# RWKV recurrence and routed experts on one core: VectorE's order of a unit, and a dV split over two engines

## The chip, the cores and the metric

The kernel runs on one core of a Trainium2 chip. Its engines take instructions in order, each from its own queue: TensorE (PE; PEld is its weight load), VectorE (DVE), ScalarE (ACT), GpSimd (POOL), and SyncE (SP), which issues most transfers. They wait for one another through semaphores. The metric is device time in microseconds (us).

## The reference

All data are float32. The first part is a recurrence over 768 steps for 4 sequences and 8 heads of 48 columns; the second sends each of the 3072 resulting rows (384 columns) to one of eight experts.

```python
for t in range(S):
    cur = np.einsum('bhd,bhe->bhde', u[None] * kt, vt)
    y[:, :, t] = np.einsum('bhd,bhde->bhe', rt, state + cur)
    state = wt[:, :, :, None] * state + np.einsum('bhd,bhe->bhde', kt, vt)
...
logits = x @ w_gate + modality_bias[modality_id]
e_idx = np.argmax(logits, axis=1)
...
    h = np.maximum(x[mask] @ w1[e], 0.0)
    out[mask] = gate_w[mask, None] * (h @ w2[e])
```

## The kernel before

**Units.** The steps are cut into chunks of 128. A unit is one chunk of one sequence with all heads: 24 units, six to a sequence. Within a unit the recurrence becomes matrix products. The decays are multiplied up from the middle of the chunk outwards, in both directions, so that K (keys) and R (receptances) carry them. Then, on TensorE: `pS` = K times R (L362), masked to the earlier steps by VectorE (`A`, L364); the state `pU` (L376), which ScalarE scales (L379) and copies (`SPb`, L382); and `pY`, the output, from the state (L392) and from A (L401). The step's own term is `delta` (L289), copied to `dT`, times v: `dV`. VectorE adds pY and dV into the row tile `xp` (`x_rows`, L427), which TensorE transposes (`x_cols`, L434) for the expert logits (L440).

**Passes.** `att_iter(i)`, i from -2 to 23, emits the work of one pass for all engines. In pass i VectorE works the scans of unit a = i + 2 (K and R), the mask of unit m = i + 1 and the rows of unit z - 1 = i - 1; TensorE works pK, pS, delta and pU of unit m and pY of unit z = i; GpSimd prepares unit a + 1. The order of the Python lines is the order of each engine's queue. GpSimd's work in a pass is: `decays` (products of neighbouring decays into `pw`, L249), `keys` (`G` = r times k, L254), `dV` of unit z (L324), `within` (two in-place products of `in`, the K half first, L267). `on_vec(n, k)` says for which units VectorE does without a product by GpSimd: there `spread` takes three operations (L273 to L275) instead of one (L277). That is so for units 0 and 1, and for K in the six `busy` passes 15 to 20. In these, GpSimd issues the scatters of the first twelve units, two to a pass (L655), and ScalarE makes dV head by head (`half_dv`, L314, four heads to a call).

**Buffers.** `BE`, in which a scan leaves its result, lies in PSUM, and so do `pY`, `pS` and `T["R"]` (`pR`, logits and the routing's small tables). pY and pS have one buffer each: pS of the next unit can be written when the mask has read it, pY of the next when `x_rows` has. `in` has four buffers, K two, R, G and pw three.

**Setup and routing.** Small pieces run at the ends of passes as `hooks`: `setup_a` to `setup_d` and `guesses` in passes 2 to 6 (biases of the two modalities, and a guess which two experts come first), the routing of the first twelve units in passes 13 to 17 (`route_a`, `hook_b` with `route_b`, `table(0)`). `hook_b` emits the rank matmuls (L499) ahead of L401 and VectorE's ranks (L509 to L515); after it the scatters may start. `split_some` in the last two passes prepares the first expert's weights.

**Experts.** The first two blocks of 512 rows are loaded when the twelve scatters have landed (`blk_load`), transposed (`blk_t`, L687) and worked by TensorE in three passes of split precision (L701, L718). Work of the second half's routing runs in between.

Of the kernel before, what the change touches and what calls it, by code (L numbers as in the profile page):

```python
# [9 lines left out]
F32 = mybir.dt.float32  # L10
# [4 lines left out]
ALU = mybir.AluOpType  # L15
# [3 lines left out]
P = 128  # L19
# [34 lines left out]
GW = B * H * S * D // (P * NG)  # L54
WHALF = FC // 2 * DM
DRAIN_FROM = WB
NEARLY = 2
SCATTER = NJ + 3
EARLY = 6
NPW = 3  # L60
# [3 lines left out]
def kernel(ctx: ExitStack, tc: tile.TileContext, rkw, vt, wf, cst, mid, wg, bias, w1, w2, out):  # L64
# [111 lines left out]
    m1 = cp.tile([P, 2, NU], F32, name="m1")  # L176
    bt2 = raw[0][:, 0, 0:NU * E].rearrange("p (a e) -> p a e", a=NU)
    bv = bb.rearrange("p (a e) -> p a e", a=2)
    mx = cp.tile([P, 2], F32, name="emx")
    ec = cp.tile([P, 2, E], F32, name="ec")  # L180

    def setup_a():
        nc.scalar.copy(out=trib, in_=mask)
        nc.scalar.copy(out=mf, in_=mi[:, 0:2 * P:2])
        nc.scalar.copy(out=ersb[0:1], in_=ers[0:1])
        nc.scalar.copy(out=rcol(C_VEC + 3 * E, 1), in_=zt[:, 0:1])
        nc.gpsimd.tensor_copy(out=tidi, in_=tid)

        nc.vector.tensor_reduce(out=mx, in_=bv, axis=AX.X, op=ALU.max)
        nc.vector.tensor_tensor(out=ec, in0=bv, in1=mx[:, :, None].to_broadcast([P, 2, E]), op=ALU.is_equal)  # L190
        nc.gpsimd.tensor_tensor(out=ec, in0=ec, in1=i8[:, None, :].to_broadcast([P, 2, E]), op=ALU.mult)

    def bias_part(s, t):
        nc.gpsimd.tensor_tensor(out=t, in0=m1[:, s, :, None].to_broadcast([P, NU, E]),
                                in1=bb[:, None, s * E:(s + 1) * E].to_broadcast([P, NU, E]), op=ALU.mult)

    def setup_b():

        pm = rcol(C_VEC, NU)
        nc.tensor.transpose(out=pm, in_=mf, identity=ident[0:NU, 0:NU])  # L200
        nc.scalar.copy(out=m1[:, 1], in_=pm)
        nc.gpsimd.tensor_scalar(out=m1[:, 0], in0=m1[:, 1], scalar1=-1.0, scalar2=1.0, op0=ALU.mult, op1=ALU.add)
        bias_part(0, biasT)
        nc.vector.tensor_reduce(out=em, in_=ec, axis=AX.X, op=ALU.min)
        for ef, eo, op in ((e0f, oh0, ALU.min), (e1f, oh1, ALU.max)):
            nc.vector.tensor_tensor(out=ef, in0=em[:, 0:1], in1=em[:, 1:2], op=op)
            nc.gpsimd.tensor_tensor(out=eo, in0=ef.to_broadcast([P, E]), in1=i8, op=ALU.subtract)
            nc.gpsimd.tensor_tensor(out=eo, in0=eo, in1=eo, op=ALU.mult)
            nc.gpsimd.tensor_scalar(out=eo, in0=eo, scalar1=-1.0, scalar2=1.0, op0=ALU.mult, op1=ALU.add)
            nc.gpsimd.tensor_scalar(out=eo, in0=eo, scalar1=0.0, scalar2=None, op0=ALU.max)  # L210
            nc.gpsimd.tensor_scalar(out=ef, in0=ef, scalar1=float(E), scalar2=None, op0=ALU.add)
        nc.gpsimd.tensor_copy(out=e0i, in_=e0f)

    def guesses():
        ts, tt = nc.gpsimd.tensor_scalar, nc.gpsimd.tensor_tensor
        ts(out=row0, in0=e0f, scalar1=float(RS), scalar2=-float(DUMMY), op0=ALU.mult, op1=ALU.add)
        nc.vector.tensor_tensor(out=thr, in0=e0f, in1=e1f, op=ALU.is_equal)
        ts(out=row1, in0=thr, scalar1=float(BW), scalar2=-float(DUMMY), op0=ALU.mult, op1=ALU.add)
        ts(out=em[:, 0:1], in0=e1f, scalar1=float(RS), scalar2=None, op0=ALU.mult)
        tt(out=row1, in0=row1, in1=em[:, 0:1], op=ALU.add)  # L220
        ts(out=tab[:, 2, 1:2], in0=thr, scalar1=-1.0, scalar2=1.0, op0=ALU.mult, op1=ALU.add)
        ts(out=thr, in0=thr, scalar1=1.0, scalar2=None, op0=ALU.add)
        nc.gpsimd.tensor_copy(out=tab[:, 0, 1:2], in_=e1f)
        nc.gpsimd.tensor_copy(out=tabe[:, 1:2], in_=e1f)
# [22 lines left out]
    def decays(n, eng):  # L247
        w = sides(ins[n % NIN][:, 1024:LIN])
        eng.tensor_tensor(out=heads(pw[n % NPW])[:, :, 2:SEG - 1], in0=w[:, :, 0], in1=w[:, :, 1], op=ALU.mult)  # L249
# [6 lines left out]
    def busy(i):  # L256
        return SCATTER <= i < SCATTER + NJ // 2

    def on_vec(n, k):
        return n < NEARLY or (k == 1 and busy(n - 2))  # L260

    def within(n):
        t = ins[n % NIN]
        for k in (1, 0):
            if not on_vec(n, k):
                v = sides(t[:, 512 * k:512 * (k + 1)])[:, :, 1 - k]
                nc.gpsimd.tensor_tensor(out=v, in0=v, in1=sides(t[:, 1024:LIN])[:, :, k], op=ALU.mult)  # L267

    def spread(n, tag, src, c0, bufs=None):
        X = sides(wt(n, tag, [P, 4, P], bufs).rearrange("p a b -> p (a b)"))  # L270
# [11 lines left out]
    def ok(n):  # L282
        return 0 <= n < NU
# [21 lines left out]
    def rows_op(a):  # L305
        scan(pw[a % NPW], 1)
        spread(a, "R", ins[a % NIN][:, 0:512], 1, 3)

    def att_iter(i):
# [4 lines left out]
                nc.scalar.activation(out=dV[:, h], in_=v0[:, h], func=AF.Copy, scale=dT[:, h:h + 1])  # L314

        if ok(a + 1):
            if a + 1 >= NEARLY:
                decays(a + 1, nc.gpsimd)
            keys(a + 1)
        if ok(z):  # L320
            dV = wt(z, "dV", [P, H, D], 2)
            v0, dT = T["v", z].rearrange("p (a b) -> p a b", a=H), T["dT", z].rearrange("p a b -> p (a b)")
            if not busy(i):
                nc.gpsimd.tensor_tensor(out=dV, in0=v0, in1=dT[:, :, None].to_broadcast([P, H, D]), op=ALU.mult)  # L324
        if ok(a + 1):
            within(a + 1)
        if ok(z - 1):
            x_rows(z - 1)
        if ok(a):
            t, W = ins[a % NIN], wt(a, "W", [P, 4], 2)  # L330
            if a < NEARLY:
                decays(a, nc.vector)
            pp, n = pw[a % NPW], 4 * SEG
            scan(pp, -1)
            spread(a, "K", t[:, 512:1024], 3)
            nc.vector.reciprocal(out=pp[:, 1:n:SEG], in_=BE[:, 2:n:SEG])
            nc.vector.tensor_copy(out=W, in_=BE[:, 2:n:SEG])
            if a < NEARLY:
                rows_op(a)
        if ok(m):  # L340
            K, R, v = T["K", m], T["R", m], T["v", m]
            last, cont = first(m + 1), not first(m)
            if not last:
                pK = pt(("k", m), "pK")
                for p in range(4):
                    nc.tensor.transpose(out=pK[:, p * P:(p + 1) * P], in_=K[:, p], identity=ident)
                if m < NEARLY:
                    warm(NWARM[1 + 2 * m])
                nc.scalar.copy(out=KT, in_=pK.rearrange("p (a h b) -> p a h b", a=4, h=2))
        if ok(z - 2):  # L350
            x_cols(z - 2, pt(("x", z), "pX" if i == NU - 1 else "pT"))
        if ok(z) and busy(i):
            half_dv(0)
        if i == SCATTER:
            route_x(0)
        if ok(m):
# [8 lines left out]
            delta(m)  # L365
            if m == 0:
                warm(NWARM[2])
        if NEARLY <= a < NU:
            rows_op(a)
        if ok(m) and not last:  # L370
            if not cont:
                T["U"] = pt(m, "pU", (P, 4, D))
# [24 lines left out]
        if ok(z):  # L397
            for h in range(H):
                p, hh = divmod(h, 2)
                for q in (0, 64):  # L400
                    nc.tensor.matmul(out=pY[q:q + 64, h * D:(h + 1) * D], lhsT=A[:, hh, p, q:q + 64], rhs=v[:, h * D:(h + 1) * D],  # L401
                                     start=(first(z) and h == 0), stop=True, skip_group_check=True)
            if busy(i):
                half_dv(1)
        if i > SCATTER:
            split_some(i)

# [111 lines left out]
    def table(ph):  # L519
# [56 lines left out]
        if ph == 0:  # L576
            rounded(g, ct, 1.0 / BW, -0.5 + 0.5 / BW)
            s0 = wt("s", "s0", [P, 2], 1)
            vec.scalar_tensor_tensor(out=fA, in0=g, scalar=1.0, in1=oh0, op0=ALU.min, op1=ALU.mult)
            vec.tensor_reduce(out=s0[:, 0:1], in_=fA, axis=AX.X, op=ALU.add)  # L580
            ts(out=tab[:, 1, 0:1], in0=s0[:, 0:1], scalar1=row0, scalar2=float(DUMMY), op0=ALU.mult, op1=ALU.add)
            yield
            vec.scalar_tensor_tensor(out=sA, in0=g, scalar=thr, in1=oh1, op0=ALU.is_ge, op1=ALU.mult)
            vec.tensor_reduce(out=s0[:, 1:2], in_=sA, axis=AX.X, op=ALU.add)
            ts(out=tab[:, 1, 1:2], in0=s0[:, 1:2], scalar1=row1, scalar2=float(DUMMY), op0=ALU.mult, op1=ALU.add)
            tt(out=fA, in0=fA, in1=sA, op=ALU.add)
            return
        if ph == 1:
            rounded(g, ct, 1.0 / BT, -0.5 + 0.5 / BT)
            vec.scalar_tensor_tensor(out=g, in0=fA, scalar=-2.0, in1=g, op0=ALU.mult, op1=ALU.add)  # L590
            sums(cu, g)
            taken(sA, cu, 1)
            ts(out=fA, in0=fA, scalar1=2.0, scalar2=None, op0=ALU.mult)
            yield
            yield from rows(SA, 1, cu, None, fA)
            tt(out=fA, in0=fA, in1=sA, op=ALU.add)
            ts(out=sA, in0=fA, scalar1=0.5, scalar2=None, op0=ALU.mult)
            return
# [500 lines left out]
```

## Time and profile before

| | |
|---|---|
| median of 3 runs | 364.48 us (364.15 to 364.69) |
| the profiled execution | 364.56 us |
| its span, first to last instruction | 362.3 us |
| mean granted TensorE clock | 0.993 |
| busy: PE, PEld | 347.5 us (96%), 314.1 us (87%) |
| busy: DVE, ACT, POOL | 234.5 us, 193.3 us, 154.4 us |

Rows of the order of time give start and length in us, engine, line, operation, `out<-in` by the program's names, the shape, and how many instructions are merged in the row; in brackets stands the idle time of the engine before it and what ended it. A VectorE instruction's length overlaps the next one's start a little, so costs in a chain are read from start to start. Rows of stretches give, after the bounds and the length, each engine's busy time, the granted clock, the DMA share and GB/s.

### The profile page before, as it was taken

How to read it: one execution, taken by the hardware profiler on the slowest of the kernel's cores; microseconds unless marked ns; L12 is line 12 of the kernel's file. 1: busy time of each engine (PE TensorE's matmuls, PEld its weight loads, DVE VectorE, ACT ScalarE, POOL GpSimd, SP SyncE). 2: the span in 40 equal slices, each digit the busy share in tenths (PEclk: the TensorE clock that was granted, in tenths of full speed). 3: DMA queues.
4: the chain of work that ended last, by engine and by line, in shares of the span. 5: the costliest groups of instructions: out<-in, count | busy, mean ns of one | idle time of the engine just before them, and what ended most of it. 6: DMA issues, size and time to landing. Idle time of an engine off the chain costs nothing.

```text
span 362.3 us, 9892 instructions
## 1 busy us (share of the span) xinstructions
PE 347.5 (96%) x3900; PEld 314.1 (87%) x3900; DVE 234.5 (65%) x481; ACT 193.3 (53%) x436; POOL 154.4 (43%) x201
## 2 busy tenths in 40 slices
PE   8899889999898999999999999999999999999993
PEld 3699789999797887799889999889988998899993
DVE  7999799999998955698756276335434443535330
ACT  2464465365758764361349565439525852665340
POOL 4898999995488863013761210201210220022021
PEclk9999999999989999999999999999999999999999
DMA  7966977786676350006330543504680566020010
GB/s 252 388 218 167 305 258 240 237 301 208 238 237 218 107 177 3 0 2 240 141 145 0 198 153 90 174 0 104 243 307 2 145 217 248 1 67 27 5 44 26
DMA packets 19612, 55.53 MB, mean 153 GB/s; under 512 B 2501, under 2 KB 10603, under 8 KB 19556
## 3 DMA queue, kind: packets, MB, share of 16 engines
q1 hardware_dynamic: 16420, 45.34, 38.1%
q0 software_dynamic: 3136, 9.47, 6.9%
q8 instruction: 32, 0.52, 0.6%
q14 instruction: 24, 0.20, 0.2%
HBM read 58.69 MB, written 12.03 MB: 195 GB/s over the span
## 4 chain that ended last, share of the span: by engine, by line
PE 56%; issue 7%; DVE 6%; ACT 4%; DMA 3%; POOLq 1%; POOL 0%; DVEq 0%; ACTq 0%
PE pS_u L701 25%; PE pY_d L718 13%; PE pX_d L718 13%; DVE pX_s L303 1%; DMA xs<-xp,posT 1%; ACT pU L379 1%; DMA xl<-xs 1%; ACT dV L314 1%; PE pK_x L687 1%; PE pU_x L687 1%; ACT SPb L382 1%; DVE A L364 1%; PE pY L401 1%; PE pT_x L687 1%; DVE K L273 1%
## 5 line engine op out<-in xcount | busy, mean ns | idle before, releaser
L726 POOL DMA_INDIRECT out<-ot,xl x25 | 26.2, 1047 | 171.9 <-ACT ot L725 147.1
L244 DVE TENSOR_TENSOR wl<-raw,wh 128x768 fp32r<-128x768 f32 x56 | 52.6, 956 | 42.7 <-ACT wh L243 41.4
L706 DVE SCALAR_TENSOR_TENSOR hl<-pS_u,hh 128x512 fp32r<-128x512 f32 x48 | 33.2, 691 | 53.4 <-ACT hh L705 53.4
L705 ACT ACTIVATE hh<-pS_u 128x512 fp32r<-128x512 f32 x48 | 28.7, 598 | 62.9 <-PE pS_u L701 62.9
L701 PE MATMUL pS_u<-xh,wl 128*128 128x512 f32 (+1 forms) x168 | 61.3, 365 | 0.0
L701 PE MATMUL pS_u<-xh,wh 128*128 128x512 f32 (+1 forms) x168 | 61.0, 363 | 0.0
L701 PE MATMUL pS_u<-xo,wh 128*128 128x512 f32 (+1 forms) x168 | 60.9, 363 | 0.0
L243 ACT CAST wh<-raw 128x768 fp32r<-128x768 f32 (+1 forms) x64 | 49.4, 800 | 13.8 <-PE pX_d L718 13.8
L701 PEld LDWEIGHTS pS_u<-xo,wh 128*128 128x128 f32 x168 | 31.5, 188 | 5.4
L701 PEld LDWEIGHTS pS_u<-xh,wh 128*128 128x128 f32 x168 | 31.6, 188 | 5.1
L701 PEld LDWEIGHTS pS_u<-xh,wl 128*128 128x128 f32 x168 | 31.5, 188 | 5.2
L303 DVE TENSOR_TENSOR_SCAN pX_s<-pw,pX_s 128x268 f32<-128x268 f32 x48 | 34.1, 710 | 0.1
L362 PE MATMUL pS<-R,K 64*128 64x128 f32 x384 | 27.9, 285 | 6.2 <-DVE R L277 5.1
L254 POOL TENSOR_TENSOR G<-in 128x512 f32<-128x512 f32 x24 | 31.5, 1311 | 5.3 <-DMA in<-rkw 5.3
L655 POOL DMA_INDIRECT xs<-xp,posT x24 | 25.3, 1053 | 19.6 <-DVE xp L515 8.3
L362 PEld LDWEIGHTS pS<-R,K 64*128 64x128 f32 x384 | 23.3, 187 | 11.5 <-DVE R L277 7.5
L718 PE MATMUL pY_d<-wh,hh 128*128 128x384 f32 x96 | 33.0, 343 | 0.0
L718 PE MATMUL pX_d<-wh,hh 128*128 128x384 f32 x96 | 32.3, 337 | 0.0
L718 PE MATMUL pY_d<-wl,hh 128*128 128x384 f32 x96 | 32.3, 336 | 0.0
L718 PE MATMUL pY_d<-wh,hl 128*128 128x384 f32 x96 | 32.3, 336 | 0.0
L718 PE MATMUL pX_d<-wl,hh 128*128 128x384 f32 x96 | 32.3, 336 | 0.0
L718 PE MATMUL pX_d<-wh,hl 128*128 128x384 f32 x96 | 32.3, 336 | 0.0
(409 smaller groups left out, 708.2 us busy)
## 6 DMA issues: line engine op xcount, KB each, us to landing
raw<-w SPq DMA_DIRECT2D x28, 768.0 KB
in<-rkw SPq DMA_DIRECT2D x22, 768.0 KB
v<-vt SPq DMA_DIRECT2D x24, 192.0 KB
wg<-wf SPq DMA_DIRECT2D x8, 576.0 KB
xl<-xs SPq DMA_DIRECT2D x5, 772.0 KB
raw<-w SPq DMA_DIRECT2D x8, 384.0 KB
xs<-zt SPq DMA_DIRECT2D x8, 193.0 KB
in<-rkw SPq DMA_DIRECT2D x6, 256.0 KB
```

Source lines behind the costliest of these rows:

```text
L243: nc.scalar.copy(out=wh[k][:, sl], in_=raw[k][:, sl])
L244: (eng or (nc.vector, nc.gpsimd)[k]).tensor_tensor(out=wl[k][:, sl], in0=raw[k][:, sl], in1=wh[k][:, sl].bitcast(F32), op=ALU.subtract)
L254: nc.gpsimd.tensor_tensor(out=G, in0=t[:, 0:512], in1=t[:, 512:1024], op=ALU.mult)
L303: nc.vector.tensor_tensor_scan(out=BE[:, ::step], data0=pp[:, ::step], data1=d1[:, ::step], initial=0.0, op0=ALU.mult, op1=ALU.max)
L362: nc.tensor.matmul(out=pS[:, hh, p], lhsT=K[q, p], rhs=R[q, p], start=True, stop=True)
L655: rows_apart("xs", nc.gpsimd.indirect_dma_start(out=xs[:, :], out_offset=bass.IndirectOffsetOnAxis(ap=posT[:, n:n + 1], axis=0), in_=T["xb ...
L687: nc.tensor.transpose(out=pp[:, c - c0, j * P:(j + 1) * P], in_=xl[:, j, c * P:(c + 1) * P], identity=ident)
L701: nc.tensor.matmul(out=pp[:, i], lhsT=wsrc[0][:, f, c * P:(c + 1) * P], rhs=xsrc[:, c, 0:w], start=(n == 0), stop=(n == 3 * KC - 1))
L705: nc.scalar.activation(out=hh, in_=pp, func=AF.Relu)
L706: nc.vector.scalar_tensor_tensor(out=hl, in0=pp, scalar=0.0, in1=hh.bitcast(F32), op0=ALU.max, op1=ALU.subtract)
L718: nc.tensor.matmul(out=X["y", q, j], lhsT=hsrc[:, j * P:(j + 1) * P], rhs=wsrc[1][:, f], start=(f == 0 and n == 0), stop=(f == FC - 1 and ...
L726: ins = nc.gpsimd.indirect_dma_start(out=out[:, :], out_offset=bass.IndirectOffsetOnAxis(ap=xl[:, j, DM + 1:DM + 2].bitcast(I32), axis=0), ...
```

## The change

VectorE's order in a pass becomes: both scans of unit a with K and R, then the rows of unit i - 1, then the mask of unit i + 1 (before: rows, scan, K, mask, scan, R). `dV` is halved in every pass that is not busy: ScalarE makes heads 0 to 3, GpSimd heads 4 to 7. In busy passes ScalarE's second half moves ahead of the scaling of pU. The decay of unit 1 goes to GpSimd. R of unit 1 is prepared by GpSimd, K of unit 2 no more. The two in-place products of `within` become one instruction over both halves. In the setup, two small tiles move to PSUM, `thr` is made there instead of in `guesses`, and one sum of `table(0)` moves to `table(1)`.

```diff
-NEARLY = 2
+NEARLY = 3
@@ setup_a
+        mx = rcol(C_VEC, 2)
         nc.vector.tensor_reduce(out=mx, in_=bv, axis=AX.X, op=ALU.max)
@@ setup_b
+        e2 = rcol(C_VEC + NU + 1, 2)
         nc.vector.tensor_reduce(out=em, in_=ec, axis=AX.X, op=ALU.min)
+        nc.vector.tensor_copy(out=e2, in_=em)
+        nc.vector.tensor_tensor(out=thr, in0=em[:, 0:1], in1=e2[:, 1:2], op=ALU.is_equal)
         for ef, eo, op in ((e0f, oh0, ALU.min), (e1f, oh1, ALU.max)):
-            nc.vector.tensor_tensor(out=ef, in0=em[:, 0:1], in1=em[:, 1:2], op=op)
+            nc.vector.tensor_tensor(out=ef, in0=em[:, 0:1], in1=e2[:, 1:2], op=op)
@@ guesses
-        nc.vector.tensor_tensor(out=thr, in0=e0f, in1=e1f, op=ALU.is_equal)
@@ on_vec, within
-        return n < NEARLY or (k == 1 and busy(n - 2))
+        return n < (1, NEARLY)[k] or (k == 1 and busy(n - 2))
 
     def within(n):
-        t = ins[n % NIN]
-        for k in (1, 0):
-            if not on_vec(n, k):
-                v = sides(t[:, 512 * k:512 * (k + 1)])[:, :, 1 - k]
-                nc.gpsimd.tensor_tensor(out=v, in0=v, in1=sides(t[:, 1024:LIN])[:, :, k], op=ALU.mult)
+        t, ks = ins[n % NIN], slice(0, 1 if on_vec(n, 1) else 2)
+        if not on_vec(n, 0):
+            v = t[:, P // 2:1024 - P // 2].rearrange("p (k c j) -> p k c j", k=2, j=P // 2)[:, ks, ::2]
+            nc.gpsimd.tensor_tensor(out=v, in0=v, in1=t[:, 1024:LIN].rearrange("p (a k j) -> p k a j", a=4, k=2)[:, ks], op=ALU.mult)
@@ att_iter
         if ok(a + 1):
-            if a + 1 >= NEARLY:
-                decays(a + 1, nc.gpsimd)
+            decays(a + 1, nc.gpsimd)
             keys(a + 1)
@@
             if not busy(i):
-                nc.gpsimd.tensor_tensor(out=dV, in0=v0, in1=dT[:, :, None].to_broadcast([P, H, D]), op=ALU.mult)
+                g = slice(H // 2, H)
+                nc.gpsimd.tensor_tensor(out=dV[:, g], in0=v0[:, g], in1=dT[:, g, None].to_broadcast([P, H // 2, D]), op=ALU.mult)
@@
-        if ok(z - 1):
-            x_rows(z - 1)
         if ok(a):
             t, W = ins[a % NIN], wt(a, "W", [P, 4], 2)
-            if a < NEARLY:
+            if a == 0:
                 decays(a, nc.vector)
@@
             nc.vector.tensor_copy(out=W, in_=BE[:, 2:n:SEG])
-            if a < NEARLY:
-                rows_op(a)
+            rows_op(a)
+        if ok(z - 1):
+            x_rows(z - 1)
@@
-                if m < NEARLY:
+                if m < 2:
                     warm(NWARM[1 + 2 * m])
@@
-        if ok(z) and busy(i):
+        if ok(z):
             half_dv(0)
@@
-        if NEARLY <= a < NU:
-            rows_op(a)
+        if ok(z) and busy(i):
+            half_dv(1)
@@
-            if busy(i):
-                half_dv(1)
@@ table, ph == 0 / ph == 1
-            tt(out=fA, in0=fA, in1=sA, op=ALU.add)
             return
         if ph == 1:
+            tt(out=fA, in0=fA, in1=sA, op=ALU.add)
```

More of the change, by code (lines that the diff above doesn't have):

```diff
@@ L178 @@
     bv = bb.rearrange("p (a e) -> p a e", a=2)
-    mx = cp.tile([P, 2], F32, name="emx")
     ec = cp.tile([P, 2, E], F32, name="ec")
```

## The prediction

> **What bounds the kernel now.** I read the profiled execution's head line, then the busy time in stretches, then the order of time of single engines, and last who ended each wait. The execution took 364.56 us (its span below and 2.26 us around it), 0.08 above the median of 364.48.
>
> ```profile
> span 362.3 us, 9892 instructions
> 54.00:82.00 28.00, 27.94 (x650) 26.05 (x651) 26.32 (x50) 14.43 (x47) 28.00 (x35) 1.00 0.76 255
> ```
>
> The columns after the length are TensorE, weight loads, VectorE, ScalarE, GpSimd, then the granted clock. In the recurrence three engines are close to full, so a step can only gain where one of them stands. One pass of VectorE, and TensorE's passes beside it:
>
> ```profile
> 54.13 0.56 DVE L427 TENSOR_TENSOR xp<-pY,dV 128x384 f32<-128x384 f32 x1
> 54.61 0.71 DVE L303 TENSOR_TENSOR_SCAN pX_s<-pw,pX_s 128x268 f32<-128x268 f32 x1
> 55.41 0.69 DVE L277 TENSOR_TENSOR K<-in,pX_s 128x512 f32<-128x512 f32 x1
> 56.01 0.18 DVE L336 RECIPROCAL pw<-pX_s 128x4 f32<-128x4 f32 x1
> 56.10 0.13 DVE L337 COPY W<-pX_s 128x4 f32<-128x4 f32 x1
> 56.15 1.22 DVE L364 TENSOR_TENSOR A<-pS,cs 128x1024 f32<-128x1024 f32 x1
> 57.28 0.71 DVE L303 TENSOR_TENSOR_SCAN pX_s<-pw,pX_s 128x268 f32<-128x268 f32 x1
> 58.10 0.69 DVE L277 TENSOR_TENSOR R<-in,pX_s 128x512 f32<-128x512 f32 x1
> 58.70 0.55 DVE L427 TENSOR_TENSOR xp<-pY,dV 128x384 f32<-128x384 f32 x1
> ...
> 54.06 1.16 PE L362 MATMUL pS<-R,K 64*128 64x128 f32 x16 [0.84 <-DVE R L277]
> 56.46 0.86 PE L392 MATMUL pY<-SPb,R 128*64 128x96 f32 x16
> 59.08 1.16 PE L362 MATMUL pS<-R,K 64*128 64x128 f32 x16
> ...
> 82.61 1.16 PE L362 MATMUL pS<-R,K 64*128 64x128 f32 x16
> ```
>
> VectorE's pass is 58.70 - 54.13 = 4.57 us: rows 0.48, scan 0.80, K 0.60, reciprocal 0.09, W 0.05, mask 1.13, scan 0.82, R 0.60, all start to start. TensorE's full pass is 59.08 - 54.06 = 5.02; passes at a sequence's ends are shorter, and six take 82.61 - 54.06 = 28.55, 4.76 each. Its pY product (L392) comes 2.40 into the pass and 2.62 ahead of the next pS.
>
> How the recurrence meets the experts:
>
> ```profile
> 90.37 0.86 PE L392 MATMUL pY<-SPb,R 128*64 128x96 f32 x16
> 91.26 0.50 PE L499 MATMUL pR_x<-oh,onesb 128*128 128x96 bf16 x12
> 93.41 0.26 DVE L509 TENSOR_TENSOR pR_x<-pR_x,oh 128x96 f32<-128x96 f32 x1
> 94.89 1.20 POOL L655 DMA_INDIRECT xs<-xp,posT  x1 [8.35 <-DVE xp L515]
> 123.33 0.97 POOL L655 DMA_INDIRECT xs<-xp,posT  x1 [0.31 <-issue]
> 132.48 0.66 PE L687 MATMUL pK_x<-cs,xl 128*128 128x128 f32 x4 [0.67 <-DMA xl<-xs]
> ```
>
> GpSimd's first scatter waits for VectorE's ranks of pass 15 (L509 starts 1.48 before it), the twelfth goes out 28.44 later behind GpSimd's own products, and the first expert's transposes wait for it 9.15 more. All that follows is TensorE's. So the end moves with the first scatter.
>
> **The change, part by part.** Passes are numbered by i.
>
> *New order on VectorE.* The second scan now follows W at once, while today the mask stands between:
>
> ```profile
> 8.51 0.72 DVE L303 TENSOR_TENSOR_SCAN pX_s<-pw,pX_s 128x268 f32<-128x268 f32 x1
> ...
> 10.40 0.18 DVE L336 RECIPROCAL pw<-pX_s 128x4 f32<-128x4 f32 x1
> 10.49 0.13 DVE L337 COPY W<-pX_s 128x4 f32<-128x4 f32 x1
> 10.65 0.72 DVE L303 TENSOR_TENSOR_SCAN pX_s<-pw,pX_s 128x268 f32<-128x268 f32 x1
> ...
> 9.66 1.28 POOL L254 TENSOR_TENSOR G<-in 128x512 f32<-128x512 f32 x1 [1.53 <-DMA in<-rkw]
> ```
>
> W to scan is 0.16 here against W to mask 0.05, since the scan needs the reciprocal's result and overwrites what W reads: 0.11 more, 4.68 a pass (0.05 below, nothing, if it hides). R, needed by the next pS, leaves VectorE earlier, and one wait on it (0.84 above) can go. What is late next is the rows operation: it starts 3.07 into the pass instead of 0, and pY has one buffer, so TensorE's next L392 must wait for it, with all TensorE work queued behind.
>
> *The start.* Unit 1's decay goes to GpSimd, which was idle from 8.13 to 9.66: done at 8.86 if an early decay costs what L249 costs below. VectorE's scan of unit 1 starts at 8.88, not 8.51. Its K stays in three operations (scan to reciprocal 1.89 instead of 1.40), its R becomes one, and unit 2's K becomes three. Passes -1 and 0 are each 1.89 + 0.09 + 0.16 + 0.82 + 0.60 + 1.13 = 4.69, so pass 1 starts at 18.26. Its rows operation runs 21.33 to 21.88. TensorE's pS of unit 2 follows unit 1's mask at 18.3, its L392 could go at 20.7 and waits till 21.95, so the next pS is at 24.57 and that of unit 4 at 29.59.
>
> *Setup.* These rows hold what happens next:
>
> ```profile
> 27.69 1.16 PE L362 MATMUL pS<-R,K 64*128 64x128 f32 x16
> ...
> 32.18 0.22 POOL L202 TENSOR_SCALAR m<-m 128x24 f32<-128x24 f32 x1 [0.23 <-ACT m L201]
> 36.00 0.73 POOL L249 TENSOR_TENSOR pw<-in 128x256 f32<-128x256 f32 x1
> 36.69 1.32 POOL L254 TENSOR_TENSOR G<-in 128x512 f32<-128x512 f32 x1
> 37.93 0.87 POOL L324 TENSOR_TENSOR dV<-v,dT 128x384 f32<-128x384 f32 x1
> 38.72 1.46 POOL L267 TENSOR_TENSOR in<-in 128x256 f32<-128x256 f32 x2
> 38.83 0.56 DVE L427 TENSOR_TENSOR xp<-pY,dV 128x384 f32<-128x384 f32 x1 [1.81 <-POOL dV L324]
> 43.43 0.56 DVE L427 TENSOR_TENSOR xp<-pY,dV 128x384 f32<-128x384 f32 x1
> 48.00 1.45 DVE L217 TENSOR_TENSOR thr<-e0f,e1f 128x1 f32<-128x1 f32 x1
> 78.70 0.69 DVE L277 TENSOR_TENSOR K<-in,pX_s 128x512 f32<-128x512 f32 x1 [0.45 <-issue]
> 88.38 0.55 DVE L427 TENSOR_TENSOR xp<-pY,dV 128x384 f32<-128x384 f32 x1
> ```
>
> L202 waits for a copy that follows pass 3 on TensorE and ScalarE, 4.49 behind that pass's pS. With the pS at 29.59 it is at 34.08; GpSimd's small operations keep their 3.82, and unit 7's decay starts at 37.90 (36.00 today). Then decay 0.69, G 1.24, the half of dV 0.45 (between 0.4, half of 0.79 start to start, and the whole 0.79), and one in-place product at G's 1.32 (between one today, 0.73, and two, 1.46): done at 41.60. So halves and product save GpSimd some 0.5 a pass, but here it has been idle for its input and the saving covers only part of the 1.9.
>
> VectorE reaches pass 4 at 18.26 + 3 x 4.68 + 0.3 and 0.7 of setup (two and five small operations at some 0.13 each, as W) = 33.3, pass 5 at 38.0, and unit 7's K at 38.8. It waits there till 41.65, 2.85 us, and rows and mask now queue behind that K. From K to the end of the mask: 0.60 + 0.09 + 0.16 + 0.82 + 0.60 + 0.48 + 1.13 = 3.88, so pass 6 starts at 45.53. Today's starts at 43.43, its own wait of 1.81 included: 2.1 lost.
>
> *What comes back.* thr (1.45 at 48.00, a 128x1 operation that ran as long as GpSimd's products beside it) moves to the setup with a PSUM operand, and the wait of 0.45 at 78.70 for TensorE goes. Today's nine passes from 43.43 to 88.38 are 44.95 = 9 x 4.57 + 1.45 + 0.45 + 1.92, the last being first routing steps, which stay. New: 45.53 + 9 x 4.68 + 1.92 = 89.57 for pass 15, 1.2 late. TensorE keeps up: 28.55 for six passes against 28.08.
>
> *Pass 15.* K in three: +0.49. Rows of unit 14 run 93.13 to 93.69, L392 goes at 93.76, and the rank matmuls end 1.39 later (90.37 to 91.76 today), 95.15. L509 starts at 95.2, behind TensorE instead of behind R, and the first scatter at 96.68: 1.79 late.
>
> *After it.* ScalarE's four-row groups of dV move ahead of pU and end a wait:
>
> ```profile
> 111.71 0.56 DVE L427 TENSOR_TENSOR xp<-pY,dV 128x384 f32<-128x384 f32 x1 [0.47 <-ACT dV L314]
> ```
>
> Some 0.5 in each of three passes, worth nothing on the path, as GpSimd's 28.44 sets the scatters. That shortens by 0.14 (one product instead of two, in the last of these passes). In the other passes ScalarE gets four small operations more. In the stretch above it is busy 14.43 of 28 us, 2.3 idle in each of six passes, and they stand ahead of its copy of delta, for which it waits anyway: nothing. Without that cover their cost falls on pU's scaling, up to GpSimd's 0.4 for the same half. The sum of routing's fA moves into the experts' stage: 0.16 of VectorE, covered by TensorE.
>
> **The sum:** +1.79 - 0.14 = +1.65, so 366.2 for the profiled execution and 366.1 for the median.
>
> **A rule beside it.** TensorE would stand idle about 2.4 us in pass 5: L392 of pass 4 waits for the rows of unit 3 till 37.0, so pass 5's pS goes at 39.7 and its L392 could at 42.1; the rows of unit 4 end at 41.65 + 0.60 + 0.09 + 0.16 + 0.82 + 0.60 + 0.56 = 44.5. This trace has seen what may follow:
>
> ```profile
> 99.63 1.16 PE L362 MATMUL pS<-R,K 64*128 64x128 f32 x16 [1.46 <-DVE R L277]
> 100.00:106.00 6.00, 6.00 (x114) 5.82 (x111) 5.69 (x16) 2.90 (x11) 5.29 (x7) 0.72 0.83 266
> ```
>
> Behind an idle time of 1.46 us the granted clock averaged 0.72 over six us: 1.68 us of full-speed work lost. The same in pass 6 would bring pass 7's pS to 44.55 + 2.62 + 4.76 + 1.68 = 53.6 and its end to 54.8, where the mask's turn is at 45.53 + 4.68 + 3.55 = 53.8: 1.0 lost, 367.1. The Trainium skill ("TensorE: Matmul & The Clock Gate", Part 1: The HAM clock gate) has the clock fall to half after an idle window of about 3.4 us. By that rule a gap of 2.4 alone would not bring it down, and the sum would stay 366.1; this trace shows the fall behind a shorter gap, so I keep it as a rival.
>
> **The rivals.**
> *GpSimd is in time (faster).* If unit 7's product is there when VectorE reaches K at 38.8, 2.85 goes and all behind it moves up: first scatter at 93.8, 1.1 early, with the 0.14: 363.2. For it: GpSimd's pass falls from 0.69 + 1.24 + 0.79 + 1.46 = 4.2 to 3.7. Against it: it works in order and its setup waits for a copy two engines away. Break-even is the product at about 40.0.
> *Nothing (same).* The 0.11 behind W hides and the product comes about half a microsecond sooner: 366.1 - 1.0 - 0.5 gives 364.6. For it: bounds above allow both. Against: both W-to-scan pairs of the start show 0.16.
> *The clock (slower still):* 367.1, as worked out above; it decides if the gap in pass 5 stays above 1.5 us.
>
> **How the numbers follow.** My forecast, 366.1 (its own range 365.3 to 366.9), has 0.42; the clock 0.12; nothing 0.24; GpSimd in time 0.22. A difference of 0.2% (0.73 us) is about what can be told from none. The low end 362.9 takes in the faster rival with 0.3 of its own, the high end 367.5 the clock. Slower 0.54, same 0.24, faster 0.22.
>
> **What would show it.** Right: TensorE waits on xp ahead of L392 in pass 1 (near 21 us) and pass 5; VectorE waits about 2.8 us ahead of unit 7's K for GpSimd's product, which ends near 41.6; first scatter near 96.7, and 28.3 from it to the twelfth; no wait of xp on ScalarE's dV. Wrong: a wait below 1.2 us at unit 7's K, L392 never waiting for xp, or W to scan at 0.05. What would upset it all is a first scatter that no longer follows VectorE's pass 15.

## The result, and the profile after

The changed kernel took 368.84 us, median of six runs (367.39 to 371.68), beside 364.59 for the kernel before (364.15 to 364.72): ratio 1.0134, 95% interval 1.009 to 1.0178. The kernel is slower, as forecast, but by 4.25 us instead of 1.65, and its runs spread over 4.3 us where those of the kernel before spread over 0.6. The profiled execution took 368.2 us with a span of 366.4, 4.1 above the span before.

TensorE in order of time, passes 1 and 2, then the granted clock there (the last three columns are clock, DMA share, GB/s):

```profile
18.36 1.16 PE L362 MATMUL pS<-R,K 64*128 64x128 f32 x16 [0.95 <-DVE A L364]
...
21.85 0.93 PE L392 MATMUL pY<-SPb,R 128*64 128x96 f32 x16 [1.26 <-DVE xp L425]
22.57 1.90 PE L401 MATMUL pY<-v,A 128*64 128x48 f32 x32
...
26.05 1.16 PE L362 MATMUL pS<-R,K 64*128 64x128 f32 x16
```

```profile
22.00:24.00 2.00, 2.00 (x44) 2.00 (x44) 1.56 (x2) 0.55 (x2) 2.00 (x3) 0.64 0.00 0
24.00:26.00 2.00, 2.00 (x17) 1.66 (x13) 1.80 (x5) 0.45 (x1) 1.56 (x3) 0.51 0.19 43
26.00:28.00 2.00, 2.00 (x46) 1.83 (x46) 1.64 (x3) 1.64 (x7) 0.00 (x0) 1.00 0.92 330
```

The wait for the rows of unit 0 is there, at 21.85 (forecast 21.95). What follows was not forecast: the clock falls to one half for some 3.4 us, the same 32 matmuls of L401 take 1.90 instead of the usual 1.09, and the next pS starts at 26.05 instead of 24.57. A second stretch of half clock, from 36.2 to 39.9, follows a wait of 1.35 us for rows in pass 3; it begins when the setup's copy that L202 waits for is all but done.

Then the setup, in three engines' order of time:

```profile
30.79 0.15 ACT L185 COPY pR_x<-zt 128x1 f32<-128x1 f32 x1
30.96 0.18 DVE L189 TENSOR_REDUCE pR_x<-bb 128x2 f32<-128x16 f32 x1 [2.48 <-ACT pR_x L185]
31.27 0.71 DVE L304 TENSOR_TENSOR_SCAN pX_s<-pw,pX_s 128x268 f32<-128x268 f32 x1
31.43 0.22 POOL L191 TENSOR_TENSOR ec<-ec,cs 128x16 f32<-128x16 f32 x1 [5.87 <-DVE ec L190]
...
42.56 1.26 POOL L268 TENSOR_TENSOR in<-in 128x512 f32<-128x512 f32 x1
43.85 0.69 DVE L278 TENSOR_TENSOR K<-in,pX_s 128x512 f32<-128x512 f32 x1 [1.79 <-POOL in L268]
```

VectorE stands 2.48 us ahead of mx until ScalarE has written a single column of the same PSUM bank: that copy is queued behind ScalarE's scaling and copies of pU. GpSimd waits 5.87 for what comes behind mx. Unit 7's product is done at 43.8 instead of 41.6.

The scatters and the first expert's transposes:

```profile
98.69 1.20 POOL L653 DMA_INDIRECT xs<-xp,posT  x1 [7.45 <-DVE xp L513]
102.43 0.88 PE L392 MATMUL pY<-SPb,R 128*64 128x96 f32 x16 [1.78 <-DVE xp L425]
126.99 0.97 POOL L653 DMA_INDIRECT xs<-xp,posT  x1 [0.30 <-issue]
135.91 0.60 PE L685 MATMUL pK_x<-cs,xl 128*128 128x128 f32 x4
```

First scatter 98.69: 3.80 after that of before, 2.01 after the forecast. From it to the twelfth 28.30, as forecast. Of the 4.1 us of the span, 3.4 stand at the first expert's transposes (132.48 before); the other 0.7 are lost in the experts' stage, for a cause that is open.

On absolute times: in the first three of the four sets of runs below, the kernel before took 376.85 to 379.35 us, with a wait of TensorE of 7.8 to 13.3 us in total between 175 and 202 us in every kernel profiled there; in the fourth it took 365.36. So ratios are each to the kernel before in the same set, and moments are counted from TensorE's pS of unit 2, which takes out a late first load. Runs in a slower state are left out of the ratios (four of c's six are), and the profiled executions of c and e8 are such runs.

### The profile page after: what moved, and what is told of

It reads as the page before. It is cut to its first block, busy times and chain, and to the rows that moved or that the text cites. A ratio compares the mean times of both kernels' runs of the same rounds, so it can differ in the third digit from the quotient of the medians.

```text
span 366.4 us, 9973 instructions
## 1 busy us (share of the span) xinstructions
PE 349.9 (95%) x3899; PEld 316.5 (86%) x3900; DVE 234.5 (64%) x481; ACT 208.4 (57%) x508; POOL 147.2 (40%) x187
## 4 chain that ended last, share of the span: by engine, by line
PE 60%; issue 7%; DVE 7%; POOLq 1%; POOL 1%; ACT 0%; DVEq 0%
PE pS_u L699 25%; PE pY_d L716 13%; PE pX_d L716 13%; DVE pX_s L304 2%; PE pY L392 2%; PE pY L401 2%; PE pS L362 1%; DVE A L364 1%; PE pK_x L685 1%; DVE xp L425 1%; PE pU_x L685 1%; POOL out L724 1%; PE pR_x L438 1%; PE pT_x L685 1%; DVE K L276 0%
## 5 line engine op out<-in xcount | busy, mean ns | idle before, releaser
L315 ACT ACTIVATE dV<-v,dT 128x48 f32<-128x48 f32 x120 | 30.4, 330 | 0.0
```

## The experiments

Theories. *Order*: rows stand behind K and R while pY has one buffer, so TensorE waits at L392, and its gaps bring the half clock. *Bank*: operands in the PSUM bank tie VectorE to ScalarE's copies. *Halves*: ScalarE's share of dV delays its own queue.

| kernel | ratio to before, interval | pS of unit 3 behind that of unit 2 | first scatter behind it |
|---|---|---|---|
| before | 1 | 4.67 | 76.89 |
| changed | 1.0134 [1.009, 1.0178] | 7.69 | 80.33 |
| e1 mx in SBUF | 1.0191 [1.0139, 1.0243] | 7.61 | 79.50 |
| e2 setup undone | 1.0122 [1.0065, 1.0178] | 8.34 | 82.52 |
| e3 rows first | 0.9932 [0.9899, 0.9965] | 4.67 | 76.47 |
| e4 before + setup | 0.9973 [0.9939, 1.0007] | 4.67 | 76.63 |
| c changed again | 1.0204 [1.0116, 1.0291] | | |
| e5 before + order | 1.0250 [1.0208, 1.0291] | 6.21 | 80.08 |
| e7 filler | 1.0159 [1.0087, 1.0232] | 6.29 | 78.97 |
| e8 rows between | 0.9925 [0.9885, 0.9965] | | |
| e13 filler, mx in SBUF | 1.0166 [1.0114, 1.0217] | 6.29 | 78.30 |
| e6 before + halves | 0.9964 [0.9920, 1.0009] | 4.66 | 76.20 |
| e9 order undone | 0.9946 [0.9913, 0.9979] | 4.67 | 75.62 |
| e12 best attempt | 0.9886 [0.9830, 0.9943] | 4.66 | 74.69 |
| c2 changed again | 1.0112 [1.0061, 1.0163] | 6.13 | 80.57 |
| e14 rows first, late passes | 1.0070 [1.0036, 1.0104] | 7.69 | 80.26 |
| e15 rows first, early passes | 0.9998 [0.9968, 1.0027] | 4.67 | 76.78 |
| e16 e13 + e14 | 1.0025 [0.9991, 1.0059] | 6.29 | 78.24 |

Where a cell is empty, the profiled execution is not compared.

### Set 1: undo one part at a time

**e1, mx in SBUF.**
```diff
+    mx = cp.tile([P, 2], F32, name="emx")
-        mx = rcol(C_VEC, 2)
```


> The changed kernel with one thing undone: the maximum of the setup (mx) lies in SBUF again instead of in the PSUM bank into which ScalarE's setup copy writes; everything else stays. Theory bank (VectorE's 2.48 us ahead of mx is a wait for ScalarE's copy into the same bank, and GpSimd's setup stands behind it): the wait goes, unit 5's first scan starts near 28.9 instead of 31.27, the second stretch of half clock (36 to 40 us) goes with TensorE's 1.35 us wait for rows, the first scatter comes 1 to 2 us earlier, 366.3 to 367.6. Theory order (rows behind K and R with one pY buffer set TensorE's pace by themselves): the wait goes, but TensorE's first gap and half clock near 22 us stay and GpSimd's setup waits as long for ScalarE's copy of pm; unit 7's K waits longer for it, and the time stays at 368.0 to 369.0. Theory halves (four more operations a pass on ScalarE): ScalarE reaches its setup copies no sooner; as order.

The wait of 2.48 goes and mx starts at 28.65, but the next bank operand takes its place. VectorE's and ScalarE's order of time:

```profile
35.54 0.18 ACT L201 COPY m<-pR_x 128x24 f32<-128x24 f32 x1
35.75 0.16 DVE L206 COPY pR_x<-em 128x2 f32<-128x2 f32 x1 [1.92 <-ACT m L201]
```

The copy e2 waits 1.92 for ScalarE's read of pm from that bank. The first scatter gains 0.8 us, less than *bank* said; the ratio (1.0191) does not fall, and lies above what either theory had. So mx's wait is real, and most of it only moves.

**e2, the whole setup undone** (mx in SBUF as in e1, thr formed in the later step again).
```diff
-        e2 = rcol(C_VEC + NU + 1, 2)
-        nc.vector.tensor_copy(out=e2, in_=em)
-        nc.vector.tensor_tensor(out=thr, in0=em[:, 0:1], in1=e2[:, 1:2], op=ALU.is_equal)
...
```


> The changed kernel with the whole setup part undone: mx in SBUF, no copy e2 in PSUM, thr formed where it was before, in the step after unit 7's pass. Theory bank: as with mx alone in SBUF, 366.3 to 367.6, and the operation thr runs 1.4 us again behind GpSimd, which shows as 0.5 to 1.2 us more than with mx alone in SBUF if VectorE is the bound there, and as nothing if TensorE's or GpSimd's lateness covers it. Theory order: 368.0 to 369.0, as every version that leaves the order.

The kernel stays slower than the one before (1.0122), as *order* said. How much the setup costs is not to be read here: in the profiled execution the clock stayed at 0.50 from 22 to 28.5 us, two such stretches on end, which makes the first scatter late, and thr ran 0.15 us, not 1.4.

**e3, rows first.**
```diff
+        if ok(z - 1):
+            x_rows(z - 1)
         if ok(a):
             t, W = ins[a % NIN], wt(a, "W", [P, 4], 2)
...
             rows_op(a)
-        if ok(z - 1):
-            x_rows(z - 1)
```


> The changed kernel with one thing undone: the rows operation stands first in VectorE's pass again, ahead of the scan, while the mask stays last. Theory order: TensorE's waits for rows ahead of its pY product (seven, 7.2 us in all) go, the clock keeps 1.00 between 20 and 40 us, pS of unit 3 starts near 24 instead of 26.05, ScalarE reaches the setup copies about 2 to 3 us sooner so that mx waits below 0.7, and the time is 363.2 to 364.9, not above the kernel before. Theory bank: mx still waits 1.5 us or more, 366 or above. Theory halves: 366 or above too, as ScalarE has the same work.

This one move takes the kernel from slower to slightly faster than before. TensorE's waits up to 140 us, the changed kernel and then e3 (total, times, longest):

```profile
PE pY L392 <- DVE xp L425: 7.2, 7, 1.8
PE pS L362 <- DVE A L364: 1.8, 2, 0.9
```

```profile
PE pS L362 <- DVE A L364: 5.2, 8, 1.0
```

No wait for rows is left. mx is in the bank as before, and it does not wait any more, since ScalarE's copy comes in time: *bank*, as a cause by itself, falls.

**e4, the setup part put into the kernel before.**
```diff
+        mx = rcol(C_VEC, 2)
...
+        e2 = rcol(C_VEC + NU + 1, 2)
+        nc.vector.tensor_copy(out=e2, in_=em)
+        nc.vector.tensor_tensor(out=thr, in0=em[:, 0:1], in1=e2[:, 1:2], op=ALU.is_equal)
...
-        nc.vector.tensor_tensor(out=thr, in0=e0f, in1=e1f, op=ALU.is_equal)
```


> The kernel before with the setup part of the change alone: mx in the PSUM bank, thr formed in the setup from a copy in PSUM. Theory order: VectorE reaches mx near 27.05 and ScalarE's copy ends at 27.56, so the wait is some 0.5 us only; the operation thr of 1.45 us near 48 goes; the time is 363.2 to 364.6. Theory bank: the bank costs by itself, the wait is above 1 us and the time 365 or above.

mx waits 0.44 (0.5 expected by *order*). The interval just includes 1: no cost of the part by itself is seen.

### Set 2: the order alone, and TensorE's gap

**c, the changed kernel again.** No edit.

> The changed kernel once more, unaltered, as the measure for the variants on the same chip. Every theory: ratio 1.009 to 1.018 to the kernel before, first scatter 98 to 99, TensorE's clock near one half for about 4 us from 22 us on.

1.0204, above the 1.018 that was expected at most, but from two runs; all six went from 381.63 to 389.32.

**e5, the order alone in the kernel before.**
```diff
-        if ok(z - 1):
-            x_rows(z - 1)
...
             nc.vector.tensor_copy(out=W, in_=BE[:, 2:n:SEG])
-            if a < NEARLY:
-                rows_op(a)
+            rows_op(a)
+        if ok(z - 1):
+            x_rows(z - 1)
...
-        if NEARLY <= a < NU:
-            rows_op(a)
```


> The kernel before with the order alone: the second scan and R follow W at once, then rows, then the mask; setup, dV and the in-place products stay as before. Theory order: TensorE waits for rows ahead of its pY product in pass 1 and later, its clock falls to near one half behind the first of these waits, the first scatter comes at 97.5 to 100, ratio 1.007 to 1.020. Theories bank and halves: nothing of theirs is in it, ratio 0.997 to 1.003.

All of the loss is in it: 1.0250, first scatter 3.2 us later than before. TensorE waits for rows in pass 1, but here the clock stays at 1.00 behind that gap, against what was expected; it falls at the longer one of pass 5 (0.91 over 40 to 60 us). So the order costs 3.2 us here without a half clock in pass 1 and without mx in the bank; GpSimd has the whole of dV and two products here, so the prediction's sum is not for this kernel.

```profile
21.58 0.88 PE L389 MATMUL pY<-SPb,R 128*64 128x96 f32 x16 [1.33 <-DVE xp L424]
44.09 1.54 PE L389 MATMUL pY<-SPb,R 128*64 128x96 f32 x16 [2.10 <-DVE xp L424]
```

**e7, filler in pass 1.**
```diff
+            if m == 2:
+                wf2 = pt('w2', 'pT')
+                for k in range(6):
+                    nc.tensor.matmul(out=wf2, lhsT=wm[:, 0:P], rhs=wm, start=(k == 0), stop=(k == 5))
             delta(m)
```


> The changed kernel with six filler products (128 x 512, bf16, into a tile that nothing reads) put ahead of the product of delta in pass 1, so that TensorE has work where it stood idle for 1.26 us waiting for rows; nothing else is changed. Theory order with the clock (the gap brings the half clock, and this the lateness of pass 2): the granted clock stays at 1.00 from 22 to 26 us, pS of unit 3 starts at 24.5 to 25.2 instead of 26.05, the first scatter comes 0.7 to 2 us earlier, ratio 1.002 to 1.010. Theory order without the clock (the rows alone set the pace): the clock stays up but the first scatter moves by less than 0.5 us, ratio as the changed kernel.

```profile
19.59 1.47 PE L368 MATMUL pT_w<-wm 128*128 128x512 bf16 x6
...
24.79 1.16 PE L362 MATMUL pS<-R,K 64*128 64x128 f32 x16
```

```profile
22.00:24.00 2.00, 2.00 (x61) 1.95 (x58) 1.69 (x2) 1.53 (x7) 2.00 (x3) 1.00 0.10 36
24.00:26.00 2.00, 2.00 (x27) 1.71 (x29) 1.66 (x5) 1.74 (x6) 1.71 (x3) 1.00 0.49 115
```

With 1.47 us of useless work the first scatter comes 1.4 us earlier than in the changed kernel: the clock stays up, and pS of unit 3 comes where the prediction had it (6.29 behind unit 2's; 24.57 - 18.3 = 6.27). So the half clock was a cost of its own. The ratio, 1.0159, is above the 1.002 to 1.010 expected; it lies below c's, inside the intervals, so what the filler gains is shown in the trace alone.

**e8, rows between.**
```diff
             nc.vector.tensor_copy(out=W, in_=BE[:, 2:n:SEG])
-            rows_op(a)
         if ok(z - 1):
             x_rows(z - 1)
+        if ok(a):
+            rows_op(a)
```


> The changed kernel with the rows operation moved to the middle of VectorE's pass, between W and the second scan. Theory order: rows now end 2.2 us into the pass, before TensorE reaches its pY product at 2.4, so TensorE waits for them nowhere above 0.3 us, the clock stays up, and the scan behind finds its reciprocal long done, so that the 0.16 us from W to scan go; the ratio is 0.988 to 0.998, as with rows first (0.993) or a little below. Theory bank or halves: 1.005 or above, since mx and the halves are as in the changed kernel.

A little faster than before, and not to be told from e3. TensorE still waits for rows three times (0.88 at most; I had said 0.3), in passes where VectorE itself is late.

### Set 3: what is left, and the other parts

**e13, both unforeseen costs out.** The edits of e1 and e7 together.

> The changed kernel with both costs taken out that the prediction had not in its sum: the six filler products in pass 1 (TensorE keeps its clock) and mx in SBUF (VectorE doesn't wait for ScalarE's copy). What is left is what the prediction worked out. If its working is right apart from these two: pS of unit 4 at 29.6 to 29.9, L202 4.49 behind it (34.1 to 34.4), unit 7's decay at 37.9 to 38.3, its in-place product done at 41.5 to 42.0, first scatter at 96.4 to 97.2, ratio 1.003 to 1.010. If something else was missed too, the first scatter stays above 97.4, as with the filler alone (97.47), ratio 1.010 or above.

Counted from pS of unit 2, the first scatter is at 78.30; the prediction's numbers give 96.68 - 18.3 = 78.38. By the clock it stands at 97.48, over the bound I had set, because this execution's pass 0 began late (unit 1's R waits 1.43 for GpSimd instead of 0.62). The ratio stays at 1.0166, far above 1.010: a loss behind the first scatter is missing in the sum. The trace has it behind the twelfth scatter:

```profile
101.22 1.55 PE L396 MATMUL pY<-SPb,R 128*64 128x96 f32 x16 [1.78 <-DVE xp L429]
...
125.72 0.98 POOL L657 DMA_INDIRECT xs<-xp,posT  x1 [0.30 <-issue]
139.47 0.60 PE L689 MATMUL pK_x<-cs,xl 128*128 128x128 f32 x4
```

The transposes come 13.75 us behind it, where the prediction had 9.15, and the clock is down (0.66 over 100 to 105 us) behind the 1.78 us that TensorE waits for rows in pass 16. In sets 1 to 3 every kernel with rows late in these passes has 12.3 to 13.75 there, every other one 8.0 to 8.9. Set 4 takes this part by itself.

**e6, dV halved in the kernel before** (and `half_dv(1)` ahead of pU).
```diff
+                g = slice(H // 2, H)
+                nc.gpsimd.tensor_tensor(out=dV[:, g], in0=v0[:, g], in1=dT[:, g, None].to_broadcast([P, H // 2, D]), op=ALU.mult)
-        if ok(z) and busy(i):
+        if ok(z):
             half_dv(0)
...
```


> The kernel before with the division of dV alone: GpSimd makes four of eight rows' groups in every pass, ScalarE the other four, and in the busy passes all eight ahead of pU. Theory halves (ScalarE's extra second a pass delays pU's scaling and the setup copies): ratio 1.004 or above, first scatter after 95.5. Theories order and bank: none of it reaches the path, ratio 0.996 to 1.003, first scatter 94.5 to 95.1; GpSimd's dV falls from 0.8 to 0.5 us and rows no longer wait for ScalarE's dV in the busy passes.

0.9964, first scatter 94.31 (94.5 expected at best). GpSimd's dV falls to 0.51. *Halves* falls as a cause of loss.

**e9, the order wholly undone.** Rows first as in e3, and `rows_op(a)` behind the mask again for a of 2 and more.

> The changed kernel with the whole order of VectorE's pass as before (rows, scan, K, reciprocal, W, mask, scan, R); setup, halves and in-place product stay changed. Theory order: as with rows first, 0.988 to 0.998; whichever of the two is lower tells whether the second scan ahead of the mask brings anything. If the scan right behind W costs (0.16 against 0.05 us), this one is lower by up to 0.002; if R's earlier end helps TensorE's pS, higher by up to 0.004. Theories bank and halves: 1.005 or above.

0.9946: what the other parts bring is hidden in the changed kernel. e3 and e9 cannot be told apart, so the second scan ahead of the mask neither helps nor hurts visibly.

**e12, an attempt at the best.** e8, mx in SBUF, and
```diff
-        return n < (1, NEARLY)[k] or (k == 1 and busy(n - 2))
+        return n < (1, NEARLY)[k] or n == 7 or (k == 1 and busy(n - 2))
```


> An attempt at a version better than both: the changed kernel with rows between W and the second scan, mx in SBUF, and K and R of unit 7 made by VectorE alone (three operations each, 0.49 more each), so that VectorE doesn't wait 1.67 us for GpSimd's product of unit 7, which stands behind its setup chain. Theory order: the wait goes, 0.98 is paid for it, first scatter 93.3 to 94.0 (94.21 with rows between alone), ratio 0.988 to 0.994. If another wait takes its place (unit 7's decay, also behind the setup chain), first scatter 94.0 to 94.6 and the ratio as with rows between alone, 0.9925.

```profile
19.78 0.18 DVE L335 RECIPROCAL pw<-pX_s 128x4 f32<-128x4 f32 x1
19.88 0.13 DVE L336 COPY W<-pX_s 128x4 f32<-128x4 f32 x1
19.93 0.55 DVE L426 TENSOR_TENSOR xp<-pY,dV 128x384 f32<-128x384 f32 x1
20.39 0.71 DVE L304 TENSOR_TENSOR_SCAN pX_s<-pw,pX_s 128x268 f32<-128x268 f32 x1
...
93.21 1.20 POOL L654 DMA_INDIRECT xs<-xp,posT  x1 [6.97 <-DVE xp L514]
```

0.9886, first scatter 93.21: faster than both kernels. With rows behind W the step from W to the next operation is 0.05 again instead of 0.16.

### Set 4: what is lost behind the first scatter

**c2, the changed kernel again.** No edit.

> The changed kernel unaltered, as the measure for the three beside it on the same chip. Every theory: ratio 1.009 to 1.025, twelfth scatter to the first expert's transposes 8.9 us or, on a chip with the added stalls, about 13.5.

In this execution the same gap of 1.26 us in pass 1 left the clock at 1.00; it fell only behind that of pass 3 (0.83 over 30 to 40 us). Its first scatter is no earlier for that (80.57): here the half clock begins early enough to delay the copy that L202 waits for (L202 5.88 behind the pS of unit 4, 5.25 in the changed kernel), and later TensorE stands 0.95 us, at 67.3, with no releaser named. The transposes come 8.94 behind the twelfth scatter.

**e14, e15, rows first in a part of the passes.** The diff is that of e14; e15 has `i < SCATTER` in both places.
```diff
+        if ok(z - 1) and i >= SCATTER:
+            x_rows(z - 1)
...
-        if ok(z - 1):
+        if ok(z - 1) and not (i >= SCATTER):
             x_rows(z - 1)
```


> The changed kernel with rows first in the pass from pass 15 on alone, as before; passes -2 to 14 keep the changed order. Theory (the order costs twice: at the start through the gap, the half clock and the setup; and again in the busy passes, where TensorE waits 1.78 us for rows and has no time to spare): first scatter within 0.7 us of the changed kernel's, counted from the pS of unit 2, but the first expert's transposes come 8 to 9 us behind the twelfth scatter, and the ratio is 0.005 to 0.013 below that of the changed kernel beside it. Rival (all of the loss is made before the first scatter): no less than the changed kernel by 0.003.

> The changed kernel with rows first in passes -2 to 14 alone, the changed order from pass 15 on. Theory (the order costs twice): first scatter as with rows first in all passes (76.5 behind the pS of unit 2), but TensorE still waits about 1.8 us for rows in pass 16 and its passes run late, ratio 0.003 to 0.012 above rows first in all (0.993). Rival (all of the loss is made before the first scatter): 0.991 to 0.996.

Early passes mended: 1.0112 to 0.9998. Late ones mended: 1.0112 to 1.0070, a little less than expected and within the intervals. In e14 TensorE is once more ahead of the data at the transposes, as before the change, and they come 8.38 behind the twelfth scatter; in e15 the gap only moves to pass 15, and the clock falls behind it (0.50 over 95 to 100 us):

```profile
134.81 0.66 PE L687 MATMUL pK_x<-cs,xl 128*128 128x128 f32 x4 [0.79 <-DMA xl<-xs]
```

```profile
92.34 0.88 PE L394 MATMUL pY<-SPb,R 128*64 128x96 f32 x16 [1.98 <-DVE xp L427]
```

**e16, only the predicted costs left.** The edits of e1, e7 and e14.

> The changed kernel with the filler in pass 1, mx in SBUF, and rows first from pass 15 on: of the order's costs only those that the prediction had in its sum are left. If its working holds, counted from the pS of unit 2 the first scatter is at 77.8 to 78.5 (the prediction: 96.68 - 18.3 = 78.4), the twelfth 28.2 to 28.4 later, the transposes 8 to 9 behind it, and the ratio is 1.001 to 1.007 (the prediction: 366.2 / 364.56 = 1.0045). If a loss was missed that lies elsewhere, 1.010 or above.

```profile
29.87 1.16 PE L364 MATMUL pS<-R,K 64*128 64x128 f32 x16
...
34.35 0.21 POOL L202 TENSOR_SCALAR m<-m 128x24 f32<-128x24 f32 x1 [1.89 <-ACT m L201]
38.16 0.72 POOL L251 TENSOR_TENSOR pw<-in 128x256 f32<-128x256 f32 x1
40.58 1.26 POOL L268 TENSOR_TENSOR in<-in 128x512 f32<-128x512 f32 x1
...
96.80 1.20 POOL L659 DMA_INDIRECT xs<-xp,posT  x1 [7.48 <-DVE xp L519]
125.07 0.98 POOL L659 DMA_INDIRECT xs<-xp,posT  x1 [0.31 <-issue]
```

The prediction had 29.59, 34.08, 37.90, the product done at 41.60 (here 41.84), 96.68, and 28.3 to the twelfth (28.27). The ratio is 1.0025 [0.9991, 1.0059]; the prediction's 366.2 over 364.56 is 1.0045. So the working describes this kernel. The changed kernel has two costs more up to the first scatter, and a third behind it whose size differs from execution to execution.

## Why the prediction was right or wrong

**Right.** The mechanism: rows late, one pY buffer, TensorE waiting at L392, its lateness carried through ScalarE's copy, GpSimd's setup and unit 7's product to the first scatter; 4.49 from pS of unit 4 to L202 (4.48 in e16); W to scan 0.16 in the changed order; the half dV 0.50, one product 1.26; 28.3 between the scatters. Rows no longer wait for ScalarE's dV, and that is worth nothing.

**Wrong, the step "The start" and the rule beside it.** The gap of 1.25 us in pass 1 was worked out, and the trace of before showed a low clock behind 1.46, yet I put the clock at pass 5 alone, as a rival with 0.12. It fell in pass 1. In five of the changed order's seven profiled executions with a gap of 1.26 to 1.33 in pass 1 the clock was halved behind it, in two it was not; in none of the eleven kernels (the one before among them) in which rows were early there or the filler stood in the gap did it fall between 20 and 28 us. With the filler the first scatter comes 1.4 us earlier. The gap of pass 5, which the rival needed above 1.5 us, was 0.66 in the changed kernel and 1.18 in e16. The spread of the changed kernel's runs fits: its two runs above 371 us have mean clocks of 0.968 and 0.977, the other four 0.985 to 0.990. In which passes those two lost it is not shown.

The Trainium skill ("TensorE: Matmul & The Clock Gate", Part 1: The HAM clock gate) has a free-running window of about 3.4 us, of which one idle window halves the clock. The length and the play of chance agree: the half clock lasted 3.4 us in the changed kernel and 6.8 in e2 and c. That the whole window must be idle does not agree: 1.26 us of waiting sufficed, perhaps with the 0.95 ahead of the pS of unit 2. The measurement decides, and by it a gap well under the window is no safe one.

**Wrong, the step "Setup".** Seven small operations were costed at 0.13 each, and their new operands in PSUM at nothing. They tie VectorE to ScalarE: 2.48 us in the changed kernel, 1.92 at the next operand in e1. Undone beside the filler (e7 to e13) mx is worth 0.7. The rest is covered, since VectorE waits for unit 7's product anyway; and so that wait was 1.79, not the 2.85 forecast, even with mx and the clock put right (1.77 in e16, where the copy e2 had waited 1.01 before). The Trainium skill ("PSUM — Partial Sum Buffer", PSUM bank collisions raise a hardware error) says that software keeps two engines apart in one bank and quadrant, even at different addresses. The row agrees: mx and ScalarE's column do not overlap, and VectorE still waited 2.48 us. Both are columns of one tile, and no run here tells a wait by bank from a wait by tile.

**Wrong, "All that follows is TensorE's".** The prediction took the 9.15 from the twelfth scatter to the transposes as fixed by the data. That was true before the change, when TensorE waited 0.67 for data there. In the changed order TensorE waits up to 1.78 for rows in the busy passes and arrives last (135.91, no wait). In the first result this added nothing to the forecast: 8.92. In sets 1 to 3 it made 12.3 to 13.75. In c, e5, e7 and e13 the clock was down over 100 to 105 us (0.66 to 0.86); in e1 and e2 it was not, so it is not the clock alone. Mending those passes alone lowers the ratio from 1.0112 to 1.0070, whose intervals overlap; the traces show that TensorE's lateness is the cause, its size is open.

**The sum**, at the first scatter: forecast +1.79, measured +3.80, so 2.01 were missing. Clock and bank together are 80.33 - 78.30 = 2.03 (the changed kernel against e13). One at a time, the filler is worth 1.36 (the changed kernel against e7) or 1.20 (e1 against e13), mx 0.83 or 0.67; each figure is from one execution of each kernel. The rival on the other side, GpSimd in time, did not happen with this order; e3, e8 and e9 show that the change's other parts would have brought 0.5 to 0.8%, and e12 1.1% with its further edits.

## What to carry to other kernels

When an operation is moved back in an engine's pass, look first at the buffer that it frees: with a single buffer, its consumer's engine stands still, and that engine's clock may fall for longer than the gap. Move it only as far as its consumer's turn allows, here between W and the second scan. And count a small operand in a shared PSUM bank as a possible wait on every engine that works in that bank, not only as an operation of 0.1 us: mx waited 2.48 in the changed kernel, 0.44 in e4 and nothing in e3.

## What the hardware showed that I had not expected

- TensorE's clock halved for 3.4 us (twice 6.8) behind gaps of 1.26 us, in five of seven executions of that order; with 1.47 us of filler it stayed up in all three.
- A reduction of 0.18 us waited 2.48 for another engine's write to other columns of its PSUM bank.
- In three sets of runs TensorE waited 7.8 to 13.3 us between 175 and 202 us, whatever the kernel, and in the fourth not at all. The row of e3 names no releaser, others VectorE's `hl`, which waited for ScalarE in its turn (e6); the cause is open.

```profile
185.03 0.80 PE L699 MATMUL pS_u<-xh,wh 128*128 128x512 f32 x1 [7.63 <-issue]
```
